# Planning TensorE work by array form in a fused attention and wave-mixing kernel

One core of a Trainium2 chip; no other core runs. The metric is the device time of one execution in microseconds, lower is better. Every ratio below is the mean time of one kernel's fast runs over that of the other's fast runs of the same rounds, so it isn't quite the ratio of the medians quoted beside it.

## The reference

Eight batches, eight heads, 576 tokens, head size 64, model size 512. Cut to what matters:

```python
kv  = einsum('bhsd,bhse->bhde', k, v)
out = einsum('bhsd,bhde->bhse', q, kv)
x   = out / sqrt(mean(out*out, -1) + 1e-6) * g_norm        # heads side by side: (8, 576, 512)
theta = x @ w_theta
y = w_tok_r @ (x*cos(theta)) + w_tok_i @ (x*sin(theta))     # over tokens
u = x + y
result = u + maximum(u @ w_ch, 0)
```

576 tokens are four full tiles of 128 and a **tail of 64**. Nearly everything that the change touches comes from that tail and from the heads of 64 columns.

## The kernel before

The kernel isn't written in the order in which it runs. Each piece of work is a task with its engines, an assumed cost, a due date, what it needs and the buffers it uses; a list scheduler walks a model of the engines, picks the next task, and emits its instructions. The engines then run their queues in that order.

```python
    def run(self):
        ...
                for (e, cost, lat, port) in engines:
                    start = max(free[e], at + self.MARGIN[e], port_free if port else 0.0)
                    ...
                    best.setdefault(e, []).append((start, due, ...))
            ...
            for (e, c) in best.items():
                first = min(x[0] for x in c) + self.SLACK[e]     # who can start about now
                (start, due, ...) = min((x for x in c if x[0] <= first), key=lambda x: (x[1], x[0]))
```

So among the tasks that could start now, the one due first is taken. "warm" tasks are matmuls without use, taken when nothing else is ready, until 72.6 us of the plan. The tasks on TensorE (PE) come in three array forms. Full: theta (`th`), mixing (`y`), channel products (`vps`), most transposes. Column halves, two products of 64 output rows side by side: `kv` of batches 2 to 7, and the tails of `raw`, `th`, `ups` and `vps`. Quadrants: `kv` of batches 0 and 1. The tails' transposes take 64 rows and so stand in a fourth form, row halves:

```python
            for kc in range(NK):                       # turn x; rows is 64 for the tail
                nc.tensor.matmul(
                    t[:, kc, :], st[f"x{b}_{ti}"][0:rows, kc * P:(kc + 1) * P],
                    ident16[0:rows, 0:rows], is_transpose=True, start=(kc == 0), stop=(kc == NK - 1))
        ...
        weave.add(("kv", b, hp), [pe(0.8 if b >= QUAD else 1.2)], ...)
        weave.add((th,), [pe(0.87 if full else 0.56)], ...)
```

The transposes of q are done by PE for batches 0 to 2 and by DMA for the others (`Q_DMA = 3`).

The **norm chain** of a token tile is `raw` (PE), `sq` (ScalarE, ACT), `ss` (VectorE, DVE), `rt` (GpSimd, POOL), `x` (DVE), `xTps` (PE), `xT` (ACT), and then `th`.

Of the kernel before, what the change touches and what calls it, by code (L numbers as in the profile page):

```python
# [9 lines left out]
FP32 = mybir.dt.float32  # L10
FP16 = mybir.dt.float16
# [7 lines left out]
PERIOD = 25.97  # L19
START = 4.0  # L20
DUE = {
    "load": (-5.25, 8.21),
    "theta": (-0.25, 0),
    "mixers": (16.85, 6.09),
    "wch": (29.24, 6.18),
    "wT": (21.53, 1.37),
    ("phase", 0): (18.6, 0.41),
    ("mix", 0): (28.29, 4.77),
    ("channel", 0): (33.17, 8.26),
    ("phase", 1): (11.06, 3.64),  # L30
    ("mix", 1): (32.1, 5.47),
    ("channel", 1): (54.19, 11.32),
    ("first", 1): (-21.36, 0.03),
    "first": (-8.71, 0),
    "cast": (24.0, 1.46),
    "turn_q": (-14.96, 0.38),
    "attention": (-4.52, 2.35),
    "norm": (6.64, 2.8),
    "turn": (-0.22, 0.91),
    "phase": (18.27, 3.54),  # L40
    "mix": (51.38, 3.12),
    "channel": (67.54, 4.04),
# [9 lines left out]
Q_DMA = 3  # L52
# [3 lines left out]
WCH_AFTER = 7  # L56


class Weave:
# [8 lines left out]
    SLACK = {"PE": 0.059, "ACT": 0.031, "DVE": 0.084, "POOL": 0.1, "SP": 0.05}  # L68
    MARGIN = {"PE": 0.004, "ACT": 0.006, "DVE": 0.569, "POOL": 0.1, "SP": 0.0}
    LANES = 8  # L70
    BEGIN = {"PE": 1.6, "ACT": 3.2, "DVE": 1.7, "POOL": 2.5, "SP": 0.73}
    WARM = 72.6
    COLD = 5.0
    URGENT = 4.1
    AHEAD = 0.13
# [19 lines left out]
    def run(self):  # L95
# [3 lines left out]
        hot, streak = False, self.BEGIN["PE"]  # L99
# [21 lines left out]
        while ready:  # L121
            best = {}
            for t in ready:
                (name, engines, due, fn, needs, makes, uses, dma) = t
                if any(not self.slots[tag] for (tag, _) in makes):
                    continue
                at = max([done[n] for n in needs], default=0.0)
                for (tag, _) in makes:
                    at = max(at, min(self.slots[tag]))
                if dma is not None:  # L130
                    at = max(at, landed[-self.LANES])
                for (e, cost, lat, port) in engines:
                    start = max(free[e], at + self.MARGIN[e], port_free if port else 0.0)
                    if name[0] == "warm" and start > self.WARM:
                        continue
                    if due < self.URGENT:
                        start = max(free[e], start - self.AHEAD)
                    best.setdefault(e, []).append(
                        (start, due, max(at, port_free) if port else at, t, cost, lat, port)
                    )  # L140
            picks = []
            for (e, c) in best.items():
                first = min(x[0] for x in c) + self.SLACK[e]
                (start, due, at, t, cost, lat, port) = min(
                    (x for x in c if x[0] <= first), key=lambda x: (x[1], x[0])
                )
                other = min(
                    (max(free[o], at) + k for (o, k, _, _) in t[1] if o != e), default=1e9
                )
                if other < max(free[e], at) + cost - 0.05:  # L150
                    start = max(start, other)
                picks.append((start, due, e, at, t, cost, lat, port))
            if not picks:
                break
            (_, _, e, at, t, cost, lat, port) = min(picks, key=lambda x: x[:3])
            (name, engines, due, fn, needs, makes, uses, dma) = t
            start = max(free[e], at)
            if e == "PE" and not hot:
                if start > free[e] + 0.4:
                    streak = start  # L160
                hot = start > streak + self.COLD
                if not hot:
                    (cost, lat) = (2 * cost, 2 * lat)
            free[e] = start + cost
            if port:
                port_free = start + cost
            end = start + lat
            if dma is not None:
                (first, took) = dma
                dma_free = max(start + first, dma_free) + took  # L170
                end = dma_free + 0.2
                landed.append(end)
            done[name] = end
            for (tag, tile_name) in makes:
                pool = self.slots[tag]
                pool.remove(min(pool))
                last[tile_name] = 0.0
            fn(e)
            for tile_name in [n for (_, n) in makes] + list(uses):
                self.users[tile_name] -= 1  # L180
                last[tile_name] = max(last[tile_name], end)
                if self.users[tile_name] == 0:
                    self.slots[self.tag[tile_name]].append(last[tile_name] + 0.05)
            ready.remove(t)
            met(("t", name))
            for (_, tile_name) in makes:
                met(("b", tile_name))
# [20 lines left out]
def kernel(  # L208
# [87 lines left out]
    wnatl = [wpool.tile([T, SF], FP16, tag=f"wnatl{i}", name=f"wnatl{i}") for i in range(2)]  # L296
    wtt = wpool.tile([P, NT, 2, T], FP16, tag="wtt", name="wtt")
    wT = {}
# [9 lines left out]
    def pe(cost):  # L308
        return ("PE", cost, cost + 0.22, False)
# [11 lines left out]
    def idle_work(n):  # L321
        name = f"warm{n}"

        def fn(e):
            t = ps("mm", [P, SH], FP32, name)
            nc.tensor.matmul(  # L326
                t[:], kv_bd[1][:, 0, :], kv_bd[1][:, 0:2, :].rearrange("p h c -> p (h c)"),
                start=True, stop=True,
            )

        weave.add(("warm", n), [("PE", 0.11, 0.11, False)], 1e6, fn, needs=[("warm", n - 1)] if n else [], makes=[("mm", name)])
# [48 lines left out]
    def load_weights():  # L380
# [38 lines left out]
        for (i, w) in enumerate((moe_w_tok_r, moe_w_tok_i)):  # L419
            for j in range(NT):  # L420
# [4 lines left out]
                cast(("wnat", i, j), name, wnat[i][:, j, :] if j < NF else wnatl[i][:],  # L425
# [25 lines left out]
    def mixer_step(n):  # L451
        name = f"wTps{n}"

        def turn(e):
            pw = st[name] = ps("tp", [P, S], FP16, name)
            for tj in range(NT):
                rows = P if tj < NF else T
                if n < 2 * NF:
                    i = n // NF
                    src = wnat[i][:, tj, :] if tj < NF else wnatl[i][:, :]  # L460
                    src = src[:, bass.ds(n % NF, P, NF)]
                else:
                    src = wtt[:rows, tj, :, :]
                nc.tensor.matmul(
                    pw[:, tj * P:tj * P + rows], src, ident16[:rows, :rows],
# [3 lines left out]
        def keep(e):  # L469
            t = wT[n] = wpool.tile([P, S], FP16, tag=f"wT{n}", name=f"wT{n}")  # L470
            if e == "ACT":
                nc.scalar.copy(out=t[:], in_=st[name][:])
            else:
                nc.vector.tensor_copy(t[:], st[name][:])

        at = due("wT", 0, n)
        weave.add(("wTps", n), [pe(0.3)], at, turn,
# [25 lines left out]
    def turn_q(b):  # L503
# [14 lines left out]
        weave.add(("qT", b, 0), [sp(1.4)], due("turn_q", b, 0), main, needs=cast,  # L518
# [4 lines left out]
    def attention(b, hp):  # L523
# [26 lines left out]
        weave.add(("kv", b, hp), [pe(0.8 if b >= QUAD else 1.2)], due("attention" if b > 1 else "first", b, hp), fn,  # L550
# [8 lines left out]
    def norm(b, ti):  # L559
# [52 lines left out]
        weave.add((raw,), [pe(0.27)], at, product, needs=qTs + bds,  # L612
# [12 lines left out]
    def turn_q_pair(b, hp, at):  # L625
# [21 lines left out]
        weave.add((pq,), [pe(0.25)], at, turn_q0, needs=[("qc", b, hp)], makes=[("tp", pq)],  # L647
# [4 lines left out]
    def by_pair(b, hp):  # L652
# [89 lines left out]
        weave.add((raw,), [pe(0.27)], at, product, needs=[("qT", b, hp), ("bd", b, hp)],  # L742
# [12 lines left out]
        weave.add((px,), [pe(0.25)], at, turn, needs=[("xp", b, hp)], makes=[(BANK["px"], px)], uses=[xn])  # L755
# [3 lines left out]
    def turn_q_tail(b):  # L759
        name = f"qTpl{b}"  # L760

        def turn(e):
            t = st[name] = ps("tp", [P, HP, T], FP16, name)
            for hp in range(HP):
                nc.tensor.matmul(
                    t[:, hp, :], qcast[b % 2][0:T, NF, 2 * hp:2 * hp + 2, :], ident16[0:T, 0:T],
                    is_transpose=True, start=(hp == 0), stop=(hp == HP - 1),
# [10 lines left out]
        weave.add((name,), [pe(0.2)], at, turn, needs=[("qcl", b)], makes=[("tp", name)],  # L778
# [4 lines left out]
    def turn_x(b, ti):  # L783
# [4 lines left out]
        def turn(e):  # L788
            rows = P if ti < NF else T
            t = st[px] = ps(BANK["px"], [P, NK, rows], FP16, px)  # L790
            for kc in range(NK):
                nc.tensor.matmul(  # L792
                    t[:, kc, :], st[f"x{b}_{ti}"][0:rows, kc * P:(kc + 1) * P],
                    ident16[0:rows, 0:rows], is_transpose=True, start=(kc == 0), stop=(kc == NK - 1),
# [34 lines left out]
        weave.add((px,), [pe(0.25 if ti < NF else 0.13)], at, turn, needs=[(f"x{b}_{ti}",)], makes=[(BANK["px"], px)],  # L829
# [5 lines left out]
    def phase(b, ti):  # L835
# [68 lines left out]
        weave.add((th,), [pe(0.87 if full else 0.56)], at, product,  # L904
# [15 lines left out]
    def mix(b, i):  # L920
# [36 lines left out]
        if open_sums:  # L957
            for ti in range(NT):
                weave.add((y, ti), [pe(0.113 * len(steps[ti]) * len(kcs))], at + 0.3 * ti,
# [5 lines left out]
        else:  # L965
            weave.add((y, NF), [pe(1.25 if half else 2.0)], at, product(0),
# [7 lines left out]
    def channel(b, ti):  # L974
# [60 lines left out]
        if pu_on:  # L1035
            weave.add((pu,), [pe(0.24 if full else 0.15)], at, turn, needs=uTs,
# [9 lines left out]
        weave.add((vp,), [pe(0.87 if full else 0.56)], at + 0.01, product,  # L1046
# [70 lines left out]
```

## Time and profile before

| | before |
|---|---|
| time, median of 3 | 226.87 us (226.05 to 226.92) |
| span of the profiled run | 224.3 us, clock 0.996 |
| PE busy | 212.9 us, 95% |
| DVE busy | 180.6 us, 81% |
| ACT busy | 155.0 us, 69% |
| changes of array form on PE | 123, of them 84 behind the kv of batch 1 |

Read the busy shares with care: the end of a matmul is modelled and matmuls overlap, so PE at 95% says that it has something in flight.

### The profile page before, as it was taken

Reading aid. Unit: us, or ns where it says so; the run is one execution under the profiler, and the core shown is the slowest. Engines: PE = TensorE matmul, PEld = TensorE weight load, DVE = VectorE, ACT = ScalarE, POOL = GpSimd, SP = SyncE. Lnnn points to the kernel's source line nnn. Section 1 sums busy time; section 2 is a strip of 40 time slices with the busy share of each in tenths; the row PEclk is TensorE's granted clock in tenths of the full one; section 3 lists DMA queues with packets and bytes.
Section 4 is the critical chain, followed back from the end, with each engine's and each line's share of the span. In section 5 each row is a group of like instructions: output and inputs, shape, how many; then the busy total and the mean of one; then the engine's idle time right before and its main releaser. Section 6 shows DMA issues by size and latency. Waiting matters only on the chain.

```text
span 224.3 us, 6007 instructions
## 1 busy us (share of the span) xinstructions
PE 212.9 (95%) x2375; PEld 146.5 (65%) x2375; DVE 180.6 (81%) x359; ACT 155.0 (69%) x302; POOL 82.7 (37%) x96
## 2 busy tenths in 40 slices
PE   7799998999999999999999999999999999999992
PEld 4666456886578566776667665676765767478561
DVE  2284728898998899879998989998979999894652
ACT  3277948985994789748796769797788777590031
POOL 6033200657004651175427555651764375100000
PEclk9999999999999999999999999999999999999998
DMA  6999999992977989998998999897852232335424
GB/s 211 379 388 271 262 364 272 290 347 74 250 241 240 206 226 225 366 207 245 215 309 181 236 273 213 228 284 208 97 109 113 77 79 42 140 94 73 158 99 164
DMA packets 61375, 47.41 MB, mean 211 GB/s; under 512 B 31524, under 2 KB 53028, under 8 KB 61348
## 3 DMA queue, kind: packets, MB, share of 16 engines
q1 hardware_dynamic: 61344, 47.04, 77.9%
q8 instruction: 18, 0.29, 0.6%
q14 instruction: 9, 0.07, 0.1%
q10 hardware_dynamic: 4, 0.00, 0.0%
HBM read 33.06 MB, written 9.44 MB: 190 GB/s over the span
## 4 chain that ended last, share of the span: by engine, by line
PE 60%; DVE 17%; POOL 11%; ACT 4%; issue 2%; DMA 2%; SPq 1%; DVEq 0%
PE y L941 20%; PE th L845 9%; PE vps L999 9%; POOL rt L591 9%; PE kv L536 6%; PE warm L326 5%; DVE x L603 4%; DVE ss L580 3%; DVE f L861 2%; PE xTps L792 2%; DMA v<-in_v_dram 2%; DVE z L898 2%; PE raw L569 2%; POOL ss L587 2%; DVE ot L1010 2%
## 5 line engine op out<-in xcount | busy, mean ns | idle before, releaser
L941 PE MATMUL y<-wT,z 128*128 128x320 f16 (+1 forms) x576 | 77.0, 286 | 0.0
L941 PEld LDWEIGHTS <-z 128*128 128x128 f16 x576 | 54.6, 98 | 16.7 <-issue 1.2
L591 POOL TENSOR_TENSOR rt<-ss,mhalf 128x8 f32<-128x8 f32 x31 | 54.9, 1771 | 2.6
L999 PE MATMUL vps<-wch,uT 128*128 128x512 f16 (+1 forms) x192 | 36.9, 344 | 0.0
L587 POOL TENSOR_SCALAR ss<-ss 128x8 f32<-128x8 f32 x31 | 9.3, 298 | 71.8 <-DVE ss L580 70.8
L952 DVE SCALAR_TENSOR_TENSOR uT<-y,gcol,xT 128x320 f16<-128x320 f32 (+1 forms) x48 | 29.1, 611 | 5.6 <-PE y L941 5.4
L845 PE MATMUL th<-wth,xT 128*128 128x512 f16 x128 | 32.3, 380 | 0.0
L801 ACT ACTIVATE xT<-xTps,gcol 128x512 f16<-128x512 f16 (+1 forms) x32 | 20.1, 629 | 14.4 <-PE xTps L792 14.0
L861 DVE SCALAR_TENSOR_TENSOR f<-pt,th 128x512 f32<-128x512 f32 (+1 forms) x40 | 24.9, 626 | 6.3 <-ACT pt L857 3.7
L857 ACT ACTIVATE pt<-th,magic_t 128x512 f32<-128x512 f32 (+1 forms) x40 | 25.6, 642 | 4.3 <-PE th L845 3.9
L536 PE MATMUL kv<-v,k 128*64 128x64 f32 (+1 forms) x672 | 26.0, 224 | 1.5 <-DMA v<-in_v_dram 1.5
L536 PEld LDWEIGHTS kv<-v,k 128*64 128x64 f32 (+1 forms) x672 | 22.4, 136 | 6.5 <-issue 3.5
L880 ACT ACTIVATE tr<-fa,pio_t 128x512 f16<-128x512 f32 x32 | 23.0, 721 | 3.3 <-DVE fa L868 3.1
L1006 ACT COPY u<-ups 128x512 f16<-128x512 f16 (+1 forms) x28 | 14.3, 518 | 15.5 <-PE ups L990 15.4
L603 DVE TENSOR_TENSOR x<-raw,rt 128x512 f16<-128x512 f32 x32 | 22.0, 687 | 3.3 <-POOL rt L591 2.7
L580 DVE TENSOR_REDUCE ss<-sq 128x8 f32<-128x512 f32 x32 | 21.5, 680 | 3.3 <-ACT sq L576 3.0
L880 ACT ACTIVATE tr<-f 128x512 f16<-128x512 f32 x32 | 20.1, 628 | 5.6 <-DVE f L861 5.4
L898 DVE TENSOR_TENSOR z<-x,tr 128x1024 f16<-128x1024 f16 (+1 forms) x32 | 19.7, 615 | 1.8 <-ACT tr L888 1.2
L999 PEld LDWEIGHTS <-uT 128*128 128x128 f16 (+1 forms) x192 | 14.4, 102 | 9.9 <-issue 0.2
L1010 DVE SCALAR_TENSOR_TENSOR ot<-vps,u 128x512 f32<-128x512 f32 (+1 forms) x28 | 17.0, 609 | 3.3 <-PE vps L999 2.3
L576 ACT ACTIVATE sq<-raw 128x512 f32<-128x512 f32 x32 | 18.6, 589 | 0.4 <-PE raw L569 0.4
L326 PE MATMUL warm<-kvbd 128*128 128x256 f16 x76 | 15.6, 294 | 3.0 <-DVE root_d L292 1.5
(99 smaller groups left out, 258.1 us busy)
## 6 DMA issues: line engine op xcount, KB each, us to landing
q<-in_q_dram SPq DMA_DIRECT2D x32, 256.0 KB, 5.4
out_dram<-ot SPq DMA_DIRECT2D x32, 256.0 KB, 3.0
k<-in_k_dram SPq DMA_DIRECT2D x24, 256.0 KB, 5.5
v<-in_v_dram SPq DMA_DIRECT2D x24, 256.0 KB, 5.9
k<-in_k_dram SPq DMA_DIRECT2D x8, 288.0 KB, 5.2
v<-in_v_dram SPq DMA_DIRECT2D x8, 288.0 KB, 6.3
wmix<-in_moe_w_tok_r_dram SPq DMA_DIRECT2D x4, 288.0 KB, 7.6
wmix<-in_moe_w_tok_i_dram SPq DMA_DIRECT2D x4, 288.0 KB, 4.8
```

The costliest lines, as they stand in the source:

```text
L326: nc.tensor.matmul(t[:], kv_bd[1][:, 0, :], kv_bd[1][:, 0:2, :].rearrange("p h c -> p (h c)"), start=True, stop=True,)
L536: nc.tensor.matmul(kvp[r * D:(r + 1) * D, hp, :], kt, vt, start=(j == 0), stop=(j == (NT if b >= QUAD else NS) - 1),)
L580: nc.vector.reduce_sum(out=t[:], in_=st[sq][:].rearrange("p (h e) -> p h e", h=H), axis=mybir.AxisListType.X,)
L591: nc.gpsimd.tensor_tensor(out=r[:], in0=t[:], in1=mhalf[:], op=ALU.pow)
L603: nc.vector.tensor_tensor(out=t[:].rearrange("p (h e) -> p h e", h=H), in0=st[raw][:].rearrange("p (h e) -> p h e", h=H), in1=st[rt][:].un ...
L845: nc.tensor.matmul(t[:], xT[:, kc, :], wth[:, kc, :], start=(kc == 0), stop=(kc == NK - 1),)
L857: nc.scalar.activation(out=t[:], in_=st[th][:], func=AFT.Identity, bias=magic_t[:])
L861: nc.vector.scalar_tensor_tensor(out=t[:], in0=st[pt][:], scalar=MAGIC, in1=st[th][:], op0=ALU.subtract, op1=ALU.subtract,)
L880: nc.scalar.activation(out=t[:, which, :], in_=src[:], func=AFT.Sin, scale=-RAD, bias=0.0 if bias is None else bias[:],)
L941: nc.tensor.matmul(st[y][:, c, :], z[:, kc * P:(kc + 1) * P], wT[m][:, cols], start=(c == 0 and m == 0) if open_sums else m == 0, stop=m = ...
L952: nc.vector.scalar_tensor_tensor(out=st["uT", b][:, chunks, cols], in0=st[y][:], scalar=gcol[:], in1=st["xT", b][:, chunks, cols], op0=ALU ...
L999: nc.tensor.matmul(t[half], uT(kc), wch[:, kc, r * n:(r + 1) * n], start=(kc == 0), stop=(kc == NK - 1),)
```

## The change

Its intent: each change of array form costs PE some time that the planner did not count as such. Now the planner counts it, prefers the form at hand, and the row-half form is done away with by turning the tails on the full array. Besides, PE transposes q of batch 3, and the dates are tuned anew. The core:

```diff
-Q_DMA = 3
+Q_DMA = 4
+    HOLD = 3.61
+    DRAIN = 0.095
+    ENTRY = {"F": 0.011, "R": 0.011, "H": 0.024, "K": 0.048, "Q": 0.048}
+    ARRAY = {"F": 0, "R": 1, "H": 2, "K": 2, "Q": 3}
...
-                    start = max(free[e], at + self.MARGIN[e], port_free if port else 0.0)
+                    new = e == "PE" and self.ARRAY[port] != form
+                    clear = free[e] + self.DRAIN if new else free[e]
+                    start = max(clear, at + self.MARGIN[e], port_free if port is True else 0.0)
...
-                        (start, due, max(at, port_free) if port else at, t, cost, lat, port)
+                        (start, due + self.HOLD * new, ..., t, cost, lat, port)
...
+            if e == "PE" and self.ARRAY[port] != form:
+                form = self.ARRAY[port]
+                start = max(free[e] + self.DRAIN, at)
+                cost += self.ENTRY[port]
...
-            t = st[px] = ps(BANK["px"], [P, NK, rows], FP16, px)
+            t = st[px] = ps(BANK["px"], [P, NK, rows], FP16 if ti < NF else FP32, px)
-                    t[:, kc, :], st[f"x{b}_{ti}"][0:rows, kc * P:(kc + 1) * P],
-                    ident16[0:rows, 0:rows], is_transpose=True, ...
+                    t[:, kc, :], st[f"x{b}_{ti}"][:, kc * P:(kc + 1) * P],
+                    ident16[:, 0:rows], is_transpose=ti < NF, ...
```

Cut: the same for the tails of q and of the mixers (with memsets of the unused rows); the tasks' PE costs (kv 0.8 to 0.58, th 0.87 to 0.866, tails 0.56 to 0.436, transposes 0.25 to 0.226); the assumed cost of a q transfer (1.4 to 3.2); all due dates, the period (25.97 to 26.33), PE's slack (0.059 to 0.141), margins and the other order numbers; the latency assumed for fillers. The old costs held a share of the price already: 0.8 us stood for a kv group that takes 0.58 us after its own form and 0.73 after the full array.

More of the change, by code (lines that the diff above doesn't have):

```diff
@@ L14 @@
 ALU = mybir.AluOpType
-PERIOD = 25.97
+PERIOD = 26.33
 START = 4.0
 DUE = {
-    "load": (-5.25, 8.21),
-    "theta": (-0.25, 0),
-    "mixers": (16.85, 6.09),
-    "wch": (29.24, 6.18),
-    "wT": (21.53, 1.37),
-    ("phase", 0): (18.6, 0.41),
-    ("mix", 0): (28.29, 4.77),
-    ("channel", 0): (33.17, 8.26),
-    ("phase", 1): (11.06, 3.64),
-    ("mix", 1): (32.1, 5.47),
-    ("channel", 1): (54.19, 11.32),
-    ("first", 1): (-21.36, 0.03),
-    "first": (-8.71, 0),
-    "cast": (24.0, 1.46),
-    "turn_q": (-14.96, 0.38),
-    "attention": (-4.52, 2.35),
-    "norm": (6.64, 2.8),
-    "turn": (-0.22, 0.91),
-    "phase": (18.27, 3.54),
-    "mix": (51.38, 3.12),
-    "channel": (67.54, 4.04),
+    "load": (-15.39, 8.44),
+    "theta": (0.94, 0),
+    "mixers": (12.3, 6.02),
+    "wch": (33.66, 6.0),
+    "wT": (20.94, 1.64),
+    ("phase", 0): (19.67, 0.63),
+    ("mix", 0): (28.29, 4.94),
+    ("channel", 0): (31.53, 7.53),
+    ("phase", 1): (11.06, 3.64),
+    ("mix", 1): (31.8, 5.47),
+    ("channel", 1): (54.0, 10.9),
+    ("first", 1): (-21.76, 0.88),
+    "first": (-9.27, 0),
+    "cast": (27.66, 1.46),
+    "turn_q": (-15.49, 0.49),
+    "attention": (-2.25, 1.53),
+    "norm": (0.56, 4.11),
+    "turn": (5.47, 0.91),
+    "phase": (18.31, 3.54),
+    "mix": (52.55, 3.41),
+    "channel": (67.54, 4.08),
 }
@@ L55 @@
 MIX_AFTER = 3
-WCH_AFTER = 7
+WCH_AFTER = 8
 class Weave:
-    SLACK = {"PE": 0.059, "ACT": 0.031, "DVE": 0.084, "POOL": 0.1, "SP": 0.05}
-    MARGIN = {"PE": 0.004, "ACT": 0.006, "DVE": 0.569, "POOL": 0.1, "SP": 0.0}
+    SLACK = {"PE": 0.141, "ACT": 0.031, "DVE": 0.084, "POOL": 0.1, "SP": 0.05}
+    MARGIN = {"PE": 0.027, "ACT": 0, "DVE": 0.564, "POOL": 0.1, "SP": 0.0}
     LANES = 8
     BEGIN = {"PE": 1.6, "ACT": 3.2, "DVE": 1.7, "POOL": 2.5, "SP": 0.73}
-    WARM = 72.6
+    WARM = 72.3
     COLD = 5.0
-    URGENT = 4.1
-    AHEAD = 0.13
+    URGENT = 5.7
+    AHEAD = 0.27
+    HOLD = 3.61
+    DRAIN = 0.095
+    ENTRY = {"F": 0.011, "R": 0.011, "H": 0.024, "K": 0.048, "Q": 0.048}
+    ARRAY = {"F": 0, "R": 1, "H": 2, "K": 2, "Q": 3}
     def __init__(self, slots):
@@ L98, in run @@
         landed = [0.0] * self.LANES
-        hot, streak = False, self.BEGIN["PE"]
+        hot, streak, form = False, self.BEGIN["PE"], 0
         loads = [name for (_, _, name) in sorted(self.loads)]
@@ L136, in run @@
                     if due < self.URGENT:
-                        start = max(free[e], start - self.AHEAD)
+                        start = max(clear, start - self.AHEAD)
                     best.setdefault(e, []).append(
-                        (start, due, max(at, port_free) if port else at, t, cost, lat, port)
+                        (start, due + self.HOLD * new, max(at, port_free) if port is True else at, t, cost, lat, port)
                     )
@@ L157, in run @@
             start = max(free[e], at)
+            if e == "PE" and self.ARRAY[port] != form:
+                form = self.ARRAY[port]
+                start = max(free[e] + self.DRAIN, at)
+                cost += self.ENTRY[port]
+                lat += self.ENTRY[port]
             if e == "PE" and not hot:
@@ L164, in run @@
             free[e] = start + cost
-            if port:
+            if port is True:
                 port_free = start + cost
@@ L172, in run @@
                 landed.append(end)
-            done[name] = end
+            done[name] = start + cost if name[0] == "warm" else end
             for (tag, tile_name) in makes:
@@ L295 @@
     wnat = [wpool.tile([P, NF, SF], FP16, tag=f"wnat{i}", name=f"wnat{i}") for i in range(2)]
-    wnatl = [wpool.tile([T, SF], FP16, tag=f"wnatl{i}", name=f"wnatl{i}") for i in range(2)]
+    wnatl = [wpool.tile([P, SF], FP16, tag=f"wnatl{i}", name=f"wnatl{i}") for i in range(2)]
     wtt = wpool.tile([P, NT, 2, T], FP16, tag="wtt", name="wtt")
+    for t in wnatl:
+        nc.gpsimd.memset(t[T:P], 0.0)
+    nc.gpsimd.memset(wtt[T:P, NF], 0.0)
     wT = {}
@@ L306, in dve, with pe @@
         return ("DVE", cost, cost + 0.14, fast)
-    def pe(cost):
-        return ("PE", cost, cost + 0.22, False)
+    def pe(cost, form="F"):
+        return ("PE", cost, cost + 0.22, form)
     def pool(n):
@@ L329, in fn @@
             )
-        weave.add(("warm", n), [("PE", 0.11, 0.11, False)], 1e6, fn, needs=[("warm", n - 1)] if n else [], makes=[("mm", name)])
+        weave.add(("warm", n), [("PE", 0.11, 0.27, "F")], 1e6, fn, needs=[("warm", n - 1)] if n else [], makes=[("mm", name)])
     def load(b, hp):
@@ L424, in load_weights @@
                       else w[SF:S, :], mixers + 0.1 + 0.1 * i + 0.01 * j)
-                cast(("wnat", i, j), name, wnat[i][:, j, :] if j < NF else wnatl[i][:],
+                cast(("wnat", i, j), name, wnat[i][:, j, :] if j < NF else wnatl[i][0:T],
                      lambda name=name, rows=rows: st[name][0:rows, 0:SF], use + i)
@@ L454, in turn @@
         def turn(e):
-            pw = st[name] = ps("tp", [P, S], FP16, name)
+            pw = st[name] = ps("tp", [P, SX], FP16, name)
             for tj in range(NT):
-                rows = P if tj < NF else T
                 if n < 2 * NF:
@@ L462, in turn @@
                 else:
-                    src = wtt[:rows, tj, :, :]
+                    src = wtt[:, tj, :, :]
                 nc.tensor.matmul(
-                    pw[:, tj * P:tj * P + rows], src, ident16[:rows, :rows],
+                    pw[:, tj * P:(tj + 1) * P], src, ident16[:],
                     is_transpose=True, start=(tj == 0), stop=(tj == NT - 1),
@@ L471, in keep @@
             if e == "ACT":
-                nc.scalar.copy(out=t[:], in_=st[name][:])
+                nc.scalar.copy(out=t[:], in_=st[name][:, 0:S])
             else:
-                nc.vector.tensor_copy(t[:], st[name][:])
+                nc.vector.tensor_copy(t[:], st[name][:, 0:S])
         at = due("wT", 0, n)
-        weave.add(("wTps", n), [pe(0.3)], at, turn,
+        weave.add(("wTps", n), [pe(0.282)], at, turn,
                   needs=[("wnat", n // NF, j) for j in range(NT)] if n < 2 * NF
@@ L517, in turn_q @@
         cast = [("qc", b, hp) for hp in range(HP)]
-        weave.add(("qT", b, 0), [sp(1.4)], due("turn_q", b, 0), main, needs=cast,
+        weave.add(("qT", b, 0), [sp(3.2)], due("turn_q", b, 0), main, needs=cast,
                   makes=[("qT", f"qT{b}")], uses=[f"qc{b}"], dma=dma(3.0))
@@ L548, in keep @@
                     nc.vector.tensor_copy(dst, src)
-        weave.add(("kv", b, hp), [pe(0.8 if b >= QUAD else 1.2)], due("attention" if b > 1 else "first", b, hp), fn,
+        weave.add(("kv", b, hp), [pe(0.58, "K") if b >= QUAD else pe(1.05, "Q")], due("attention" if b > 1 else "first", b, hp), fn,
                   needs=[("k", b, hp), ("v", b, hp)] + ([("kl", b), ("vl", b)] if b >= QUAD else []),
@@ L611, in norm @@
         bds = [("bd", b)] if b > 1 else [("bd", b, hp) for hp in range(HP)]
-        weave.add((raw,), [pe(0.27)], at, product, needs=qTs + bds,
+        weave.add((raw,), [pe(0.226, "F" if ti < NF else "H")], at, product, needs=qTs + bds,
                   makes=[(bank, raw)], uses=[f"qT{b}", f"bd{b}"])
@@ L645, in keep_q0 @@
                 nc.vector.tensor_copy(t, src)
-        weave.add((pq,), [pe(0.25)], at, turn_q0, needs=[("qc", b, hp)], makes=[("tp", pq)],
+        weave.add((pq,), [pe(0.226)], at, turn_q0, needs=[("qc", b, hp)], makes=[("tp", pq)],
                   uses=[f"qc{b}"])
@@ L741, in by_pair @@
                   uses=[kvn] + ([bdn] if hp else []))
-        weave.add((raw,), [pe(0.27)], at, product, needs=[("qT", b, hp), ("bd", b, hp)],
+        weave.add((raw,), [pe(0.226)], at, product, needs=[("qT", b, hp), ("bd", b, hp)],
                   makes=[(bank, raw)], uses=[qTn, bdn])
@@ L754, in by_pair @@
                   makes=[] if hp else [(home, xn)], uses=[raw, rt] + ([xn] if hp else []))
-        weave.add((px,), [pe(0.25)], at, turn, needs=[("xp", b, hp)], makes=[(BANK["px"], px)], uses=[xn])
+        weave.add((px,), [pe(0.226)], at, turn, needs=[("xp", b, hp)], makes=[(BANK["px"], px)], uses=[xn])
         weave.add(("xTp", b, hp), [act(SF, 1), dve(0.42, True)], at, keep, needs=[(px,), "gcol"],
@@ L762, in turn @@
         def turn(e):
-            t = st[name] = ps("tp", [P, HP, T], FP16, name)
+            t = st[name] = ps("tp", [P, HP, T], FP32, name)
             for hp in range(HP):
                 nc.tensor.matmul(
-                    t[:, hp, :], qcast[b % 2][0:T, NF, 2 * hp:2 * hp + 2, :], ident16[0:T, 0:T],
-                    is_transpose=True, start=(hp == 0), stop=(hp == HP - 1),
+                    t[:, hp, :], qcast[b % 2][:, NF, 2 * hp:2 * hp + 2, :], ident16[:, 0:T],
+                    start=(hp == 0), stop=(hp == HP - 1),
                 )
@@ L777, in turn_q_tail @@
         at = due("turn_q", b, HP) if b > 1 else due("first", b, HP - 1) - 0.1
-        weave.add((name,), [pe(0.2)], at, turn, needs=[("qcl", b)], makes=[("tp", name)],
+        weave.add((name,), [pe(0.12)], at, turn, needs=[("qcl", b)], makes=[("tp", name)],
                   uses=[f"qc{b}"])
@@ L789, in turn @@
             rows = P if ti < NF else T
-            t = st[px] = ps(BANK["px"], [P, NK, rows], FP16, px)
+            t = st[px] = ps(BANK["px"], [P, NK, rows], FP16 if ti < NF else FP32, px)
             for kc in range(NK):
                 nc.tensor.matmul(
-                    t[:, kc, :], st[f"x{b}_{ti}"][0:rows, kc * P:(kc + 1) * P],
-                    ident16[0:rows, 0:rows], is_transpose=True, start=(kc == 0), stop=(kc == NK - 1),
+                    t[:, kc, :], st[f"x{b}_{ti}"][:, kc * P:(kc + 1) * P],
+                    ident16[:, 0:rows], is_transpose=ti < NF, start=(kc == 0), stop=(kc == NK - 1),
                 )
@@ L828, in turn_x @@
             return
-        weave.add((px,), [pe(0.25 if ti < NF else 0.13)], at, turn, needs=[(f"x{b}_{ti}",)], makes=[(BANK["px"], px)],
+        weave.add((px,), [pe(0.226 if ti < NF else 0.12)], at, turn, needs=[(f"x{b}_{ti}",)], makes=[(BANK["px"], px)],
                   uses=[f"x{b}_{ti}"])
@@ L903, in phase @@
         full = ti < NF
-        weave.add((th,), [pe(0.87 if full else 0.56)], at, product,
+        weave.add((th,), [pe(0.866) if full else pe(0.436, "H")], at, product,
                   needs=([("xTp", b, hp) for hp in range(HP)] if b < 2 and full else [("xT", b, ti)])
@@ L958, in mix @@
             for ti in range(NT):
-                weave.add((y, ti), [pe(0.113 * len(steps[ti]) * len(kcs))], at + 0.3 * ti,
+                weave.add((y, ti), [pe(0.11 * len(steps[ti]) * len(kcs))], at + 0.3 * ti,
                           product(ti),
@@ L965, in mix @@
         else:
-            weave.add((y, NF), [pe(1.25 if half else 2.0)], at, product(0),
+            weave.add((y, NF), [pe(1.225 if half else 1.965)], at, product(0),
                       needs=[(f"z{b}_{ti}",) for ti in range(NT)] + [("wT", m) for m in range(NM)],
@@ L1035, in channel @@
         if pu_on:
-            weave.add((pu,), [pe(0.24 if full else 0.15)], at, turn, needs=uTs,
+            weave.add((pu,), [pe(0.226) if full else pe(0.12, "H")], at, turn, needs=uTs,
                       makes=[(BANK["pu"], pu)], uses=[f"uT{b}"])
@@ L1045, in channel @@
         us = [(u,)] if pu_on else [("ud", b, kc) for kc in range(NK)]
-        weave.add((vp,), [pe(0.87 if full else 0.56)], at + 0.01, product,
+        weave.add((vp,), [pe(0.866) if full else pe(0.436, "H")], at + 0.01, product,
                   needs=uTs + [("wch", kc) for kc in range(NK)] + ([] if pu_on else us),
```

## The prediction

> **What bounds the kernel now.** I read the page's first two parts, then the chain of waits in order of time, then the stretches table.
>
> The page says which engine is full, and when:
>
> ```profile
> PE 212.9 (95%) x2375; PEld 146.5 (65%) x2375; DVE 180.6 (81%) x359; ACT 155.0 (69%) x302; POOL 82.7 (37%) x96
> ...
> PE   7799998999999999999999999999999999999992
> ...
> DVE  2284728898998899879998989998979999894652
> ```
>
> PE is at 9 in nearly every slice from about 20 us to the end; DVE is close behind but has holes. A busy PE isn't a PE at its peak, so I looked at start to start of its matmuls. From 43 us (where the kv work of batch 1 ends) to the end PE is released late by another engine for only about 3 us in all; everything else is work, or a gap that no wait explains. The chain shows that gap:
>
> ```profile
> 58.02 0.86 PE th L845 x4
> 58.88 0.22 PE ups L990 x4
> 59.11 0.73 PE kv L536 x20
> 59.84 0.33 PE qTps2h L632 x4
> 60.17 0.86 PE th L845 x4
> 61.03 0.73 PE kv L536 x20
> 61.76 0.44 PE th L850 x8
> 62.20 0.58 PE kv L536 x20
> 62.78 1.33 PE y L941 x9
> ```
>
> The columns are start, length, engine, tile and line, count. The same 20 kv matmuls take 0.58 us after another half-array group (th L850, 128*64 in the table by form) and 0.73 us after a full-array group. Four transposes take 0.22 us after a full-array group and 0.33 us after kv. So going into a half-array group costs about 0.15 us, coming back about 0.11 us; a smaller group (raw on column halves, 0.34 us after a full group against the 0.22 us or so of its steady pitch) shows about 0.12 us. I take **0.12 us per change of array form**, a mean of these.
>
> The start is another regime, and so is what lies next to PE later:
>
> ```profile
> 20.00:36.00 16.00, 14.75 (x141) 8.47 (x140) 7.91 (x19) 11.20 (x23) 2.29 (x6) 1.00 1.02 314
> 36.00:48.00 12.00, 12.00 (x209) 10.20 (x205) 11.14 (x26) 11.66 (x26) 4.77 (x6) 1.00 1.13 283
> 48.00:200.00 152.00, 149.64 (x1640) 102.75 (x1639) 139.22 (x269) 116.68 (x220) 68.78 (x67) 1.00 0.77 196
> ```
>
> Columns: stretch, PE, PEld, DVE, ACT and POOL busy, clock, DMA. From 36 to 48 us ACT (11.66 of 12) and DVE (11.14 of 12) are full: they finish the sines and z of batch 0, on which the first y waits, while before 36 us both idle and PE runs fillers ("warm"). From 48 us on DVE is busy 139.2 of 152 us, 92%: the next bound.
>
> **What the Trainium skill says.** "TensorEngine Tiling (Array Packing)", Key Properties: changing the tiling mode, not just the tile, drains the TensorE. The trace agrees: the first matmul of a new form starts 93 to 95 ns later than the pitch explains. "TensorE: Matmul & The Clock Gate", on the 56 ns gap: a warm matmul costs N / 2.4 + 2.5 ns from start to start; this trace has 56 ns at N=128, 109 at 256, 136 at 320, 216 at 512, and 29 at 64. So a transpose of 64 columns costs the same 29 ns whether 64 or 128 rows are fed, if the formula holds for the new shape. "PSUM — Partial Sum Buffer", Specifications: a matmul writes fp32 while a transpose keeps the input's type; that is why the tails, now plain matmuls with an identity, get fp32 tiles. No trace here shows that shape yet.
>
> **The change, part by part.** I compared the order of the built programs on each engine.
>
> 1. Changes of form on PE. Before: 123, over 64 stretches of partial-array work (23 stretches begin with kv, 20 with a row-half transpose, the others with raw, ups, th or vps tails and the gain). After: 64, over 33 stretches; row halves are gone, and halves stand together (raw, kv, ups, vps and th of different batches). 59 fewer x 0.12 = 7.1 us. But only where PE is the bound does this count: after the kv of batch 1 there are 83 against 45, 38 fewer x 0.12 = **4.6 us**. The other 21 lie in the start, beside fillers and waits.
>
> 2. Added PE work. q of batch 3: 16 transposes x 56 ns + 4 x 29 ns = 1.0 us. The fifth matmul of each mixer transpose is now 128 wide: 9 x 27 ns = 0.24 us, mostly in the start. Tails of x and q: unchanged at 29 ns each. Summing the pitches over the work that stands behind batch 1's kv gives 163.0 us before and 165.0 after: 1.1 us of the above, and 0.9 us that moved there from before it. So from that point PE needs 4.6 - 2.0 = **2.6 us less**.
>
> 3. Start. Loads of batch 1's first pair now stand between the four theta chunks, so the weights come some 830 KB later, at the 380 GB/s of that stretch about 2.2 us. In return its q, kv and norm are done while PE and ACT had nothing to do; fillers fall from 76 to 42. Summing the trace's own mean durations along the new order: ACT has 30.4 us of work up to batch 0's last sine instead of 33.5; of it 8.7 us, not 11.8, stand between the first pair of sines and the last, the stretch where ACT was full. DVE has 8.7 us, not 12.1, between the first and the last z. In the timeline ACT idles 1.5, 1.4, 0.3 and 0.6 us between 29 and 35 us behind wT and qT copies that now stand elsewhere. The relief is about 3 us, later weights may eat up to 2: I put the start at **3 us less**, anywhere from 0 to 4.
>
> 4. DVE gets some 5 us more (359 to 368 instructions; qT copies 3 to 7 at 0.42 us, wT 7 to 9, xT 1 to 4, two weight casts), but all save about 1 us falls in the start, where it had room. Batch 3's two transposing transfers go; their loads' data lay 5 to 25 us ahead of use, so no gain.
>
> 5. New waits. 139.2 us plus 1 of DVE work in a stretch shortened by some 3 us is 94% instead of 92%, and a half-array task held back for company delays its followers. I charge **0.7 us**.
>
> Sum: -2.6 - 3.0 + 0.7 = -4.9 us, so **221.9 us** from 226.87.
>
> **The rivals.** *DVE takes over*: what PE no longer loses is waited for at x, f or uT. For it: 92% now, the chain between 89 and 163 us runs largely through DVE and POOL. Against it: PE itself had no slack there, and its idle before y and th groups is 0.0. Then only the start and the last 40 us gain: about 224.5. *The start gives nothing*: the later weights move th of batch 0 by 2 us and cancel the lighter ACT and DVE: about 224.5 too; both rivals together give 226 or so. *The start gives more*, because sines follow the table load at once, and the replanned order leaves fewer waits: 219. *Fewer fillers cool the clock*: granted clock is 1.00 throughout, PE is dense, and the page's clock row shows no dip; I give it little, but it would cost several us at once.
>
> **Range and chances.** The step with the largest spread is the start (0 to 4), then DVE (0.3 to 3). Together: 80% between **218.8 and 224.8**. The mark for 2% is 222.3, just above my number, so it is near to even: faster by over 2% **0.56**, within 2% **0.42**, slower **0.02**. The many retuned order numbers, which presumably were kept because they helped, tip it.
>
> **What would show it right or wrong.** Right: in the chain, kv groups of 0.58 us follow each other and the 0.33 and 0.73 us pieces become about half as many; PE matmuls x2361 (2375 - 34 fillers + 20); tail transposes stand in the full form at 29 ns pitch; batch 1's last kv no later than 44 us and its first y batch done earlier; DVE busy near 94% from 48 to 200 us. Wrong: if the pitch of the new tail matmuls, with 128 rows or fp32 output, is well above 29 ns; if a change of form still costs as much in total because each costs more; if th of batch 0 starts after 24 us and nothing is regained by 48 us; or if PE's late releases from 43 us on rise from 3 us to over 6, which would mean that DVE took the gain.

## The result

The kernel after takes **219.66 us** (219.13 to 220.94, 4 runs) against 226.52 us (226.05 to 226.92, 4 runs): ratio 0.9706, 95% interval 0.9658 to 0.9754. In another call it stood at 0.970 (219.05 us) again.

The first two parts of the page, after:

```profile
PE 206.3 (95%) x2361; PEld 145.8 (67%) x2361; DVE 182.5 (84%) x368; ACT 155.3 (71%) x304; POOL 81.4 (37%) x93
...
PE   7898888999999999999999999999999999999992
...
DVE  3197689899989899889998999999899999973652
```

PE has 6.6 us less busy time though it does more (185.4 us of matmul pitch, the steady start-to-start time, before, 186.6 after, fillers aside). The busy time is rough: a second profile of the same kernel has 203.8 us. DVE is fuller. The same stretches as in the prediction, after (PE, PEld, DVE, ACT, POOL busy, clock, DMA):

```profile
20.00:36.00 16.00, 13.53 (x157) 8.11 (x153) 12.27 (x28) 14.12 (x31) 4.75 (x8) 1.00 0.92 296
36.00:48.00 12.00, 11.53 (x177) 9.74 (x177) 10.87 (x24) 11.18 (x25) 6.07 (x6) 1.00 1.14 294
48.00:200.00 152.00, 150.72 (x1685) 106.99 (x1685) 139.50 (x271) 118.54 (x223) 65.11 (x64) 1.00 0.74 198
```

Between 20 and 36 us DVE works 12.3 us where it worked 7.9, ACT 14.1 where it worked 11.2: work was brought forward into the idle start. The chain of waits in order of time shows grouping (start, length, what):

```profile
159.46 0.73 PE kv L549 x20
160.19 0.33 PE xTps L805 x4
160.52 0.34 PE raw L582 x8
160.87 1.17 PE kv L549 x40
162.03 0.97 PE th L858 x4
```

Two kv groups follow raw tails in one stretch of column halves: 1.17 us for 40, which is 0.58 us for 20, and only the return to the full array (th 0.97 instead of 0.86) is paid.

The most telling line is the chain's summary by line for the stretch 89 to 164 us, cut off on the right as the view gives it. Before:

```profile
by line: POOL rt L591 22.9%; DVE x L603 10.0%; DVE ss L580 7.5%; DVE f L861 6.8%; DVE z L898 6.3%; PE y L941 5.3%; DVE uT L952 5.0%; issue 4.8%; POOL ss L587 4.7%; PE th L845 3.9%; DVE fa L868 3.9%; DVE ot L1010 3.8%; ACT tr L888 2.5%; PE x
```

After:

```profile
by line: PE y L954 31.7%; PE th L858 13.1%; PE vps L1012 11.8%; PE kv L549 7.8%; POOL rt L604 6.7%; PE xTps L805 4.8%; PE raw L582 4.7%; DVE x L616 3.2%; PE ups L1003 3.1%; DVE ss L593 2.5%; DVE uT L965 2.4%; POOL ss L600 2.0%; DVE z L911 1
```

Summed by engine over these 75 us (pieces cut at the window's ends): before DVE 34.8, POOL 20.7, PE 11.4; after PE 58.6, DVE 9.9, POOL 5.7. Before, the path ran through the norm chain and DVE's queue; after, it runs through PE, in the second profile too (y 31.7%, rt 4.5%). The prediction had taken PE for the bound of the old order from 43 us on.

To compare kernels of different order I use one marker: the moment at which so many microseconds of PE work (sum of matmul pitches, fillers aside) are still to come. All from single profiles:

| us of PE work left | 165 | 140 | 120 | 100 | 80 | 60 | 40 | 20 | last matmul |
|---|---|---|---|---|---|---|---|---|---|
| before | 42.4 | 69.2 | 91.1 | 112.5 | 133.9 | 156.6 | 178.7 | 199.8 | 219.9 |
| after | 40.8 | 66.9 | 88.1 | 109.5 | 130.4 | 151.2 | 172.0 | 193.2 | 213.3 |
| difference | -1.6 | -2.3 | -3.0 | -3.0 | -3.5 | -5.4 | -6.7 | -6.6 | -6.6 |

A quarter of the gain is there at 42 us, nearly half is won between 134 and 179 us, nothing after that.

### The profile page after: what moved, and what is told of

It is laid out like the page before. It is cut to its first block, busy times and chain, and to the rows that moved or that the text cites. A ratio compares the mean times of both kernels' runs of the same rounds, so it can differ in the third digit from the quotient of the medians.

```text
span 217.8 us, 5976 instructions
## 1 busy us (share of the span) xinstructions
PE 206.3 (95%) x2361; PEld 145.8 (67%) x2361; DVE 182.5 (84%) x368; ACT 155.3 (71%) x304; POOL 81.4 (37%) x93
## 4 chain that ended last, share of the span: by engine, by line
PE 63%; ACT 13%; DVE 8%; DMA 8%; POOL 4%; issue 2%; SPq 0%; DVEq 0%; ACTq 0%
PE y L954 26%; PE vps L1012 12%; PE th L858 8%; PE kv L549 5%; DMA wst<-in_moe_w_theta_dram 3%; ACT pt L870 3%; PE xTps L805 3%; DMA k<-in_k_dram 3%; ACT tr L893 3%; PE raw L582 2%; POOL rt L604 2%; PE ups L1003 2%; DVE ss L593 2%; DMA v<-in_v_dram 2%; DVE x L616 2%; ACT tr L901 2%
## 5 line engine op out<-in xcount | busy, mean ns | idle before, releaser
L604 POOL TENSOR_TENSOR rt<-ss,mhalf 128x8 f32<-128x8 f32 x31 | 54.0, 1742 | 2.6
L600 POOL TENSOR_SCALAR ss<-ss 128x8 f32<-128x8 f32 x31 | 10.5, 337 | 68.5 <-DVE ss L593 67.6
L858 PE MATMUL th<-wth,xT 128*128 128x512 f16 x128 | 31.7, 379 | 0.7 <-DVE f L874 0.7
L549 PEld LDWEIGHTS kv<-v,k 128*64 128x64 f32 (+1 forms) x672 | 24.2, 145 | 5.6 <-issue 3.7
L549 PE MATMUL kv<-v,k 128*64 128x64 f32 (+1 forms) x672 | 27.2, 232 | 0.6 <-DMA v<-in_v_dram 0.5
L593 DVE TENSOR_REDUCE ss<-sq 128x8 f32<-128x512 f32 x32 | 21.6, 680 | 2.3 <-ACT sq L589 2.1
L858 PEld LDWEIGHTS <-xT 128*128 128x128 f16 x128 | 11.4, 98 | 11.4 <-ACT xT L814 1.2
```

Of the source, the lines that this page charges most:

```text
L549: nc.tensor.matmul(kvp[r * D:(r + 1) * D, hp, :], kt, vt, start=(j == 0), stop=(j == (NT if b >= QUAD else NS) - 1),)
L593: nc.vector.reduce_sum(out=t[:], in_=st[sq][:].rearrange("p (h e) -> p h e", h=H), axis=mybir.AxisListType.X,)
L604: nc.gpsimd.tensor_tensor(out=r[:], in0=t[:], in1=mhalf[:], op=ALU.pow)
L858: nc.tensor.matmul(t[:], xT[:, kc, :], wth[:, kc, :], start=(kc == 0), stop=(kc == NK - 1),)
```

## The experiments

Twelve runs, each timed in three rounds against the kernel before on the same chip. The first was the kernel after once more, as the mark (0.970, 219.05 us; its trace is level with the first one's within 0.4 us throughout):

> The kernel after, unchanged, as the mark for the runs beside it on this chip: about 219.7 us, 0.970 of the kernel before.

### 1. Tails on the full array, in the old order

```diff
 # before.py, in the x, q and mixer tails alone; assumed costs untouched, so the plan is the same
-  st[f"x{b}_{ti}"][0:rows, ...], ident16[0:rows, 0:rows], is_transpose=True
+  st[f"x{b}_{ti}"][:, ...],      ident16[:, 0:rows],      is_transpose=ti < NF
```

> The kernel before, with its own planned order kept instruction for instruction; only the tails of x, q and mixers are turned on the full array. Changes of array form fall from 123 to 87, and from 84 to 68 after the kv of batch 1. Drain theory: the 16 late ones are worth 16 x 0.12 = 1.9 us and the 20 early ones little, so about 224.6 us. Rival (the gain lies in the new order alone, or the new tail matmuls with 128 rows and fp32 output cost more than 29 ns each): 226.5 or a little more.

The order on PE, DVE, ACT and the DMA queue was compared and is the same, instruction for instruction. Measured: 223.94 us, ratio 0.9869 (0.983 to 0.9907). It gains more than I expected (2.5 us by the medians, 3.0 by the ratio; 2.0 between the two profiles), and elsewhere. The chain, before:

```profile
26.00 0.88 PE wTps L464 x10
...
29.37 0.37 PE wTps L464 x5
```

and in this run:

```profile
26.33 0.56 PE wTps L466 x10
...
29.28 0.28 PE wTps L466 x5
```

In start-to-start times each mixer transpose loses 190 ns of the way from its fourth matmul to its successor (302 to 112 ns), and a tail of x or q between full-array groups 200 ns (531 to 332 ns from the matmul before it to the one after). That is the drain price, confirmed: some 95 ns on either side, 10 ns more inside. But by the marker the run is ahead of before by 1.5 us at 165 us of work left, 1.8 at 140, 1.7 at 60, 2.0 at the end. **Three quarters of it are won in the first 42 us**; from the last kv of batch 1 to the last matmul it takes 175.3 us instead of 175.8, so 16 changes of form taken away there are worth 0.5 us. The prediction had it the other way round. These are single profiles; where the rest of the timed gain lies they don't show.

### 2. Tails on row halves, in the new order

```diff
 # after.py, the same lines turned back; assumed costs untouched
```

> The kernel after, its planned order kept; only the tails of x, q and mixers are turned on row halves again. Changes of form rise from 64 to 102, and from 46 to 67 after the kv of batch 1. Drain theory: 21 x 0.12 = 2.5 us in the full stretch, up to 1 us in the start, so 222.2 to 223. Rival (DVE now limits, PE has slack): under 220.5.

Measured: 220.49 us, ratio 0.9748 (0.9682 to 0.9814). By the ratios that is some 1 us above the kernel after (0.9706, and 0.970), but the intervals overlap: the loss isn't clear of noise. The drains are back, as the timeline shows on the tail of q of batch 3. The kernel after:

```profile
72.23 1.03 PE L858 MATMUL th<-wth,xT 128*128 128x512 f16 x4
73.09 0.28 PE L778 MATMUL qTpl<-ident,qcast 128*128 128x64 f16 x4
73.21 1.03 PE L858 MATMUL th<-wth,xT 128*128 128x512 f16 x4
```

This run:

```profile
72.33 1.03 PE L856 MATMUL th<-wth,xT 128*128 128x512 f16 x4
73.28 0.29 PE L776 MATMUL qTpl<-ident,qcast 64*128 64x64 f16 x4
73.50 1.04 PE L856 MATMUL th<-wth,xT 128*128 128x512 f16 x4
```

From th to th 0.98 us without, 1.17 with. Summed over the tails behind the kv of batch 1 the price is about 2.0 us. From the last kv of batch 1 to the last matmul this profile takes 173.9 us instead of 172.9, so about half of it arrives; its start happened to be 0.7 us shorter, which leaves 0.3 us at the end. So my number failed and the rival's ("PE has slack, under 220.5") was closer: in this order too, a good part of an added drain is absorbed.

### 3. The planner blind to forms

```diff
-    ARRAY = {"F": 0, "R": 1, "H": 2, "K": 2, "Q": 3}
+    ARRAY = {"F": 0, "R": 0, "H": 0, "K": 0, "Q": 0}
```

> The kernel after, all parts and all dates kept, but the planner is told that every form is the same array, so it neither counts drains nor groups. 88 changes of form instead of 64, 68 instead of 46 after the kv of batch 1. Drain theory: 22 x 0.12 = 2.6 us, so about 222.3 us, more if the plan now also misses the real times. Rival (grouping costs followers as much as it saves): 219.5 to 220.5.

Measured: 225.72 us, ratio 0.9959 (0.991 to 1.0007): nearly the whole gain is lost, 6 us, more than twice what 22 drains cost. It is level with the kernel after until 120 us of work are left (88.7 against 88.1), 2.8 us behind at 60 and 7.4 at 20. There PE waits for others:

```profile
178.55 0.63 PE L863 MATMUL th<-wth,xT 128*64 128x256 f16 x8
180.23 0.40 PE L805 MATMUL xTps<-ident,x 128*128 128x128 f16 x4 [1.05 <-DVE x L616]
180.47 0.39 PE L582 MATMUL raw<-kvbd,qT 128*128 128x128 f16 x4
181.90 1.89 PE L858 MATMUL th<-wth,xT 128*128 128x512 f16 x4 [1.04 <-ACT xT L814]
```

The th group takes 1.89 us instead of about 1.0 because the granted clock was 0.5 for 3.4 us from 181.5 us on. That share (some 1.7 us) is of this one profile, the slowest of the four runs; the others lie at 225.25 to 225.8, the fastest at a clock of 1.00. So a plan that doesn't know the drains pays them and, in addition, orders the engines against each other for times that don't come. One thing wasn't separated: this planner has the new, lower costs too (kv 0.58), which leave no room for a drain, while the old blind one had 0.8. A blind planner with the old costs and these tails wasn't run.

### 4. Drains counted, no preference for the form at hand

```diff
-    HOLD = 3.61
+    HOLD = 0.0
```

> The kernel after with drains still counted by the planner but no preference for the form at hand (hold of 0 instead of 3.61 us). 82 changes of form, 64 after the kv of batch 1. Drain theory: 18 x 0.12 = 2.2 us, about 221.9 us. If it is as slow as the blind plan, grouping is what pays; if it is at 220, knowing the true times is what pays.

Measured: 221.44 us, ratio 0.9765 (0.9727 to 0.9803), 1.3 to 1.5 us above the kernel after by the ratios; the intervals overlap a little, but its four runs (221.37 to 221.93) lie above seven of the eight of the kernel after. So grouping as such is worth some 1.4 us, about what its 18 more late changes cost at near 0.1 us each. Against experiment 3 it is 4.3 us faster with 64 changes behind the kv of batch 1 instead of 68: not the number of drains but the plan that counts them parts the two, at these dates.

### 5. q of batch 3 by DMA

```diff
-Q_DMA = 4
+Q_DMA = 3
```

> The kernel after, but q of batch 3 is transposed by DMA again, all dates kept and the order planned anew. PE loses 1.0 us of transposes, ACT and DVE some 2 us of copies; changes of form after the kv of batch 1 come to 54 instead of 46 in the new order, 8 x 0.1 = 0.8 us. Prediction's account (no gain from this part as such): 219.5 to 220.5. Rival (raw of batch 3 waits for a transfer of 6 us that PE now spares it): 221.5 or more, with a wait of PE before raw of batch 3.

Measured: 223.44 us, ratio 0.9876 (0.9826 to 0.9926), outside both expectations' reasons. Its profile (225.07 us) is the slowest of its four runs, the fastest took 222.25. By the marker it is level with the kernel after while batch 3 is served and long after (88.8 against 88.1 at 120 us left, 130.3 against 130.4 at 80, 151.6 against 151.2 at 60), and loses 5.3 us only in the last 60 us of PE work, with waits of PE for z and x of the last batches. q of batch 3 is long done there; that the new plan orders the last batches worse because the dates were tuned for another plan is likely and not shown. What this part is worth when retuned stays open; up to 60 us of work left it shows neither gain nor loss.

### 6. The old dates

```diff
 # after.py with DUE, PERIOD, WCH_AFTER, WARM, URGENT, AHEAD of before.py (SLACK and MARGIN stay)
-PERIOD = 26.33
+PERIOD = 25.97
-    "load": (-15.39, 8.44),
+    "load": (-5.25, 8.21),
...
```

> The kernel after, planner aware of forms and tails on the full array, but with the due dates, period and urgency of the kernel before (the slack and margin of each engine stay new, since a slack below the drain would starve every change of form). Weights are loaded ahead of batch 1 again, as before. 56 late changes of form against 46: 10 x 0.1 = 1 us; the start back to the kv of batch 1 ending at 42 to 43 us instead of 40.4: 2 us. So 222.5 us. If the dates are worth nothing: 220.5. If they are most of the gain: 225.

Measured: 223.22 us, ratio 0.9852 (0.9825 to 0.9879). The total is near to the expectation, the reason isn't: the start is not slower. The last kv of batch 1 begins at 39.7 us (after: 40.4; before: 44.1) although the weights are loaded ahead of batch 1, and until 40 us of work are left it is within 0.9 us of the kernel after. It loses at the end: the last matmul 2.6 us later, and in the profiled run, the slowest of its four, a store that takes 4.27 us, on which the last `ot` waits.

```profile
213.44 0.70 DVE ot L1023
...
214.16 4.27 DMA out_dram<-ot
```

So the interleaved loads, on which the prediction built, aren't needed for the shorter start; and an aware planner with old dates has most of the gain until it comes to the end. In all, though, its 0.9852 is no better than the full-array tails alone in the old order (experiment 1, 0.9869): the aware plan pays only with dates that were tuned for it.

### 7. The new dates in the old planner

```diff
 # before.py with DUE, PERIOD, WCH_AFTER, SLACK, MARGIN, WARM, URGENT, AHEAD of after.py
```

> The kernel before (blind planner, row-half tails, q of batch 3 by DMA) with the dates, slack, margins and urgency of the kernel after. 97 late changes of form against 84: 13 x 0.1 = 1.3 us more, while the new load order could save up to 3 us in the start. 225 to 228 us; if the retuned dates alone were the gain, under 223.

Measured: 232.48 us, the median of three fast runs (a fourth, 236.38, was slow), ratio 1.0279 (1.0251 to 1.0307), slower than expected. The last kv of batch 1 begins at 44.3 us as before; from there on 97 changes of form and 17.3 us of gaps between matmuls (before: 12.7). The dates alone are no gain at all.

### 8. Which engine binds: four runs with less work

Two cuts, in both kernels with the order kept. Their outputs are wrong, which doesn't matter for the times. PE: one of nine mixer steps is left out of most y sums; by the pitches that is 7.4 us (the expectation said 6.9: four sums of batch 0 lose it too). DVE: each sum over a head takes half its elements; 32 sums went from 0.68 to 0.41 us each, so 8.5 us (the expectation said some 10).

```diff
-  ms = steps[ti] if open_sums else [m for step in steps for m in step]
+  ms = steps[ti] if open_sums else [m for step in steps for m in step if m != 1]
```

```diff
-  out=t[:], in_=st[sq][:].rearrange("p (h e) -> p h e", h=H),
+  out=t[:], in_=st[sq][:].rearrange("p (h e) -> p h e", h=H)[:, :, 0:D // 2],
```

> The kernel before with the same cut of 6.9 us of PE work, order kept. If PE alone binds: about 219.5. The run of before with full-array tails won nothing between 67 and 164 us, so I expect DVE, or the norm chain through DVE and POOL, to bind there: 3 to 4 us less, in the last 60 us mostly.

> The kernel before with the same cut of some 10 us of DVE work, order kept. If DVE binds between 67 and 164 us: 2 to 4 us less, gained in that stretch. If PE binds there: under 0.7 us less.

> The kernel after, order kept, wrong on purpose: one of the nine mixer steps is left out of each y from batch 1 on, so PE has 0.98 us less per batch, 6.9 us in all, evenly spread. PE alone binds after 42 us: about 213 us (6.9 less). PE and DVE bind together: 3 us less, 216.5, with the gain mainly in the last 45 us, where DVE has little to do.

> The kernel after, order kept, wrong on purpose: the sum over each head takes half of its elements, so each of 32 DVE reductions of 0.68 us takes about 0.35 us, some 10 us of DVE in all. PE alone binds: under 0.7 us less. DVE binds with PE: 2 us less or more.

| cut | median, us | ratio to before | first uT of batch 1, 3, 5, 7 against the uncut profile, us |
|---|---|---|---|
| PE 7.4 us, before | 225.27 | 0.9936 (0.9905 to 0.9966) | +0.1, +0.2, +0.2, -0.9 |
| DVE 8.5 us, before | 225.03 | 0.9919 (0.9892 to 0.9946) | +0.2, -0.2, -1.7, -1.7 |
| PE 7.4 us, after | 215.94 | 0.9523 (0.9501 to 0.9544) | -0.2, -1.5, -1.6, -3.0 |
| DVE 8.5 us, after | 217.82 | 0.96 (0.9575 to 0.9626) | -0.2, -0.7, -1.3, -1.6 |

In the kernel before, **7.4 us less on PE move nothing up to batch 6** and 1.4 us in all (226.6 x 0.0064). The freed time turns into waits. PE's longest waits from 45 us on, before (us in total, times, longest):

```profile
PE xTps L792 <- DVE x L603: 1.6, 5, 0.6
PE th L850 <- ACT xT L801: 0.7, 1, 0.7
```

with less work on PE:

```profile
PE xTps L792 <- DVE x L603: 4.3, 8, 0.8
PE th L850 <- ACT xT L801: 0.8, 1, 0.8
PE y L941 <- DVE ot L1010: 0.7, 1, 0.7
```

All gaps between matmuls behind the kv of batch 1 grow from 12.7 to 18.7 us. Nor does DVE alone bind: 8.5 us less there give 1.8, and at once the chain from 89 to 164 us runs through PE (y 32.1%, th 15.2%, vps 13.1%, rt 4.9%). In that fixed order each engine stands close behind the other. In the kernel after, about half of a cut on PE comes out at the end (3.1 to 4.0 us, by medians and by ratios against the mark). This is what the chain of waits said: the new order has PE on the path, the old one the norm chain. But PE doesn't bind alone there either: the cut on DVE brings 1.2 to 2.3 us by the same measures, no less than before.

## Why the prediction was right, and where it wasn't

**Range and direction.** 219.66 us lies in 218.8 to 224.8, and "faster by over 2%", at 0.56, came. The number, 221.9, was 2.2 us too high: 4.9 us of gain were forecast and 6.9 measured. That it came so near is in part luck, as the terms show.

**The price of a change of form** (0.12 us): right. Two lone row-half sides cost 0.19 to 0.20 us together (experiments 1 and 2), a return from column halves 0.11 us.

**The count** (123 to 64): right; 2361 matmuls as said. Behind the kv of batch 1 the traces have 84 and 46, not 83 and 45, with the same difference; of DVE's nine more instructions three, not four, are qT copies. The new tail matmuls have the 29 ns pitch that was assumed.

**"4.6 - 2.0 = 2.6 us less" on PE behind batch 1's kv, and 0.7 us of new waits.** From the last kv of batch 1 to the last matmul it took 175.8 us before and 172.9 after: 2.9 us less, against 1.9 by these two steps. The term for waits was mis-sized: gaps that are neither pitch nor fillers went from 12.7 to 7.6 us, 5.1 less, where 4.6 of drains and 0.7 more waits make 3.9. Waits did not grow; PE's idle time from 43 us on went from 2.4 to 1.3 us.

**"Only where PE is the bound does this count", and PE as the bound from 43 us on.** This step failed as a mechanism. In the old order neither 16 drains (experiment 1) nor 7.4 us of mixing (experiment 8) taken from PE shorten the stretch from 45 to 187 us by more than a few tenths. PE showed little waiting, and the prediction read that as being the bound; its own rival had named the chain through DVE and POOL from 89 to 163 us and set it aside. In the old order PE, DVE and POOL stand close behind each other. The reduction counted with a plan that was made with it: blind, the same dates and parts give 225.7 us (with the reserve named in experiment 3).

**"The other 21 lie in the start, beside fillers and waits."** Wrong: in the old order the tails' drains there, 20 changes, are worth 1.5 us of the 2.0 us that experiment 1's profile gains; there PE is on the path between two mixer transposes and the y sums.

**"The start at 3 us less."** The last kv of batch 1 begins 3.7 us earlier. The size was near, and of the reasons one held: ACT and DVE are lighter between the first sines and the last z of batch 0. From the first z to the last it took 8.6 us instead of 11.5 (forecast: 8.7 of DVE work instead of 12.1), and the last z starts 3.8 us earlier. The load order isn't needed for it (experiment 6), and the later weights cost nothing: the first th starts at 21.4 us (before: 21.6). Lighter drains were left out, though experiment 1 gains 1.5 us by them. The shift of ACT and DVE work wasn't tested alone. Experiment 2 loses nothing in the start, so with the new order there the tails no longer seem to matter to it: the two don't add up.

**DVE near 94%.** In the stretch that was named, 48 to 200 us, it is busy 139.5 of 152 us, 92% as before; that stretch now holds more of the kernel's end. From 45 us to 190 it is 136.5 of 145 us, 94%; before, from 45 to 195, 137.6 of 150, 92%. The rival "DVE takes over" fell all the same: denser DVE came with fewer waits of PE.

**Open.** What is won between 134 and 179 us is the plan's doing, for the aware plans and the blind one part ways there; which of its many decisions does it wasn't found. Experiments 5 and 6 lose 2 to 5 us in the last batches for changes that lie elsewhere, so the share of a single part in a retuned kernel can't be read from them. A rival stands untested: the dates of the kernel after were tuned for its plan, and each change of an input lost something, so a part of the gain may be the choice of a lucky order among many. A blind planner with full-array tails, tuned anew, would tell; it wasn't run.

## What to carry to other kernels

If a program's order is fixed by a plan, a cost taken away in silence may be worth little, while a plan made with the true cost may gain more than the cost itself: check with a run that keeps the order, and one that plans anew. An engine that is 95% busy with few waits isn't shown to bind; take work from it, with the order kept, and see whether the end moves. Small products on parts of the array are worth putting together, or shaping for the full array where the rows are free: here some 1.4 us (experiment 4) and 2 to 3 us (experiment 1).

## What the Trainium skill lacked or had wrong

- "TensorEngine Tiling (Array Packing)", Key Properties, says that a change of tiling mode drains but gives no cost: 93 to 96 ns on each side of a row-half tail here, 0.20 us for a lone one (531 against 332 ns from neighbour to neighbour).
- "TensorE: Matmul & The Clock Gate", Part 4, gives about 275 ns for a 128x128 transpose in one kernel's context. Here a transpose lasts 219 ns, but four in a row stand 56 ns apart, so the pitch and not the latency is what they cost.
- The same page, "HAM oscillation", has the clock halve when PE idles for more than about 3.4 us. In experiment 3 the granted clock was 0.5 for 3.4 us from 181.5 us on, though in the 3.4 us before PE idled only 1.05 and 0.66 us, with short work between; in experiment 5 for 3.4 us from 32.6 us on, after 0.59 us of idling behind fillers (ends of matmuls are modelled).
- "Perfetto Trace Analysis", Transposes, advises transpose mode over a standard matmul. For a 64-token tail the plain matmul with an identity has the same 29 ns pitch; fed with 128 rows it stands in the full form and spares the drains. Transpose mode with 128 rows and 64 columns wasn't run.
